# The last output quarter of a slot, evicted by the slot after it

## The chip, the cores and the metric

One core of a Trainium2 chip runs the kernel. The metric is the device time of one execution in microseconds (us). Three runs before the change took 793.52, 794.09 and 795.62 us, median 794.09. Five engines work side by side: TensorE (PE, matmuls), VectorE (DVE), ScalarE (ACT), GpSimd (POOL) and SyncE (SP). Each runs its own instructions in order and waits for the others at semaphores. SP issues the weight loads; POOL issues the indirect DMAs that gather token rows and scatter output rows.

## The reference

The reference first computes an attention with sigmoid weights (8 batches, 12 heads, 448 positions, head size 64), and then a mixture of experts on its 3584 rows of 768 numbers, with one expert of eight for each row:

```python
attn = 1 / (1 + exp(-(q @ k.T / sqrt(64) - log(448))));  x = attn @ v
logits = x @ w_gate;            e = argmax(logits)
gate = softmax(logits)[e];      eom = sigmoid(x @ w_output_gate)[e]
out = gate * eom * (maximum(x @ w1[e], 0) @ w2[e])     # w1: 768x1024, w2: 1024x768
```

## The kernel before

The attention fills the first 330 us or so. The rest is the mixture of experts, cut into slots. A slot is a set of token rows of one expert, and its code is one body. There are full slots of 256 tokens, wide slots of 192 (128 and a quarter of 64) and half slots of 128. Every product is made of three matmuls, with each operand split into a high part (an ACT cast) and the rest (a DVE subtraction): `split` writes both.

A full body (`slot`) runs in this order. SP's loads of the next slot's w1 (`load_slot`, issued in `load_w`, L525, three loads of 1 MB; each only where the expert changes). The split of the first fourth of w2 (L535 on ACT, L536 on DVE). Layer 1 in eight chunks of six matmul pairs (L579, L580), whose sum is evicted by ACT (L587) and DVE (L588); chunks go round three PSUM banks, 0, 1 and 2, so that the fourth chunk needs the first one's eviction. Then the next slot's rows are turned (`turn_x`, L561 on DVE), POOL gathers the rows of the slot after that (L504), the turned rows and w1 are split (L539, L542). Layer 2 makes four output quarters (t, n), t the half of the tokens and n the half of the columns, each of 24 matmuls (L604 to L606). ACT evicts each quarter with its gate as scale into the tile `ys[t]` (L616), and when n is 1 POOL scatters `ys[t]` to the output (L618, 128 rows of 3072 bytes). The list `lt` holds a slot's row numbers and gates.

A wide body is the same for 192 tokens, with the 64 in fp32 without a split: `layer2_q` (32 matmuls at L661, evicted at L663, scattered at L664) and two more quarters. A half body has another order, in which hidden units are transposed by PE (`turn`, L705) from a tile that ACT writes (L726).

Slots 0 to 3 always run. The rest sit in nested branches: `If(full > k)` with full bodies (L968), then `If(wide > k)` with wide ones (L973), then `If(part > k)` with half ones (L978). With these inputs 11 full slots run (7 inside branches), 3 wide ones and 2 half ones. Where a nest is left, each engine jumps on its own and adds what the bodies not run would have added to its semaphores. Its event there waits for all its own earlier work: on POOL for the landing of each of its DMAs, and then an instruction (INC_SWDGE_SEM) brings its DMA semaphores to the later count. What comes next on another engine waits for such a count wherever it depends on anything that a body of the nest may have done.

The order inside a body is the order of the code, engine by engine.

Of the kernel before, what the change touches and what calls it, by code (L numbers as in the profile page):

```python
# [12 lines left out]
I32 = mybir.dt.int32  # L13
# [9 lines left out]
E = 8  # L23
# [12 lines left out]
EARLY = -(-(ROWS_E - E * (TS - 1)) // TS)  # L36
# [18 lines left out]
def r32(ap):  # L55
    return ap.bitcast(F32)


class Kernel:
# [19 lines left out]
    def memory(self):  # L79
        self.rounded = self.pool("rounded").tile([128, ROUNDED // 4], F32R, name="rounded")  # L80
        self.plain = self.pool("plain").tile([128, PLAIN // 4], F32, name="plain")
        ps = self.pool("psum", space=PSUM).tile([128, 8, 512], F32, name="ps")
        self.ps_s = [ps[:, 0:2], ps[:, 2:4]]
        self.ps_o = [[ps[:, 4], ps[:, 5]], [ps[:, 6], ps[:, 7]]]
        self.mm_ps, self.mm_late = ps[:, 5], ps[:, 7]
        self.psx = [ps[:, i].rearrange("p (d t) -> p d t", d=2) for i in (6, 7)]
        self.psh = [ps[:, i] for i in (0, 1, 2, 4, 5)]
        self.psy = [ps[:, i] for i in (4, 5, 3)]
        self.rot = {}

        c = self.carve
        w = c(0, 3, 2, 2, DF)
        self.w1s = [[w[:, d // 2, a, d % 2] for d in range(6)] for a in range(2)]
        self.w1p = [[w[:, k, a] for k in range(3)] for a in range(2)]
        self.xc = c(12 * DF * 4, 6, 2, TS)
        self.xs = [self.xc[:, :, i] for i in range(2)]

        self.w1r = c(0, 6, DF, dt=F32)
        o = 6 * DF * 4
        self.xg = c(o, 8, Q4, dt=F32)  # L100
        self.xT = c(o + XG, 6, TS, dt=F32)
        o += 2 * XG
        self.w2r = c(o, 8, DM, dt=F32)
        self.li = c(o, LROWS, 6, dt=F32)
        self.lr_e = [c(o + LROWS * 24 + i * 768, 192, dt=F32, parts=32) for i in range(2)]
        self.tmp_early = o + 4096
        self.step = c(o + 8192, B, 4, dt=F32, parts=CP)
        self.tokf = c(o + 8192 + 16 * B, NCH, 4, dt=F32, parts=CP)
# [29 lines left out]
    def constants(self):  # L138
        nc = self.nc
        cp = self.const = self.pool("const")  # L140
# [20 lines left out]
            t, pattern=pattern, base=base, channel_multiplier=0, allow_small_or_imprecise_dtypes=True)  # L161
# [29 lines left out]
        nc.gpsimd.memset(self.seg, 1.0)  # L191
        nc.gpsimd.memset(self.seg[:, :, 0:1], 0.0)
        slots = EARLY + LATE_N
        self.lts = cp.tile([128, slots, 2, 2], I32, name="lts")
        self.lxs = cp.tile([128, slots, 8], I32, name="lxs")
        for i, st in enumerate((1, TS)):
# [4 lines left out]
        own = gl[1].bitcast(I32)  # L201
# [403 lines left out]
            nc.tensor.matmul(ps, hh[:, f, tk], wl, start=False, stop=False)  # L605
            nc.tensor.matmul(ps, hl[:, f, tk], wh, start=False, stop=(f == 7))  # L606

    def layer2(self, s, t, n, y):
        ps = self.take("y", self.psy)[:, 0:384]
        self.layer2_mm(ps, t, n, range(8))  # L610
        self.layer2_out(ps, s, t, n, y)

    def layer2_out(self, ps, s, t, n, y):
        nc = self.nc
        c = slice(384 * n, 384 * n + 384)
        nc.scalar.activation(y[:, c], ps, AF.Copy, scale=r32(s["lt"][:, t, 1:2]))  # L616
        if n == 1:
            nc.gpsimd.indirect_dma_start(  # L618
                out=self.out, out_offset=bass.IndirectOffsetOnAxis(ap=s["lt"][:, t, 0:1], axis=0),
                in_=y, in_offset=None, bounds_check=NT - 1, oob_is_err=False)  # L620

    def slot(self, m, side=None, drain=False):
        tab, k = (self.tab_e, m + 1) if m + 1 < EARLY else (self.tab_l, m + 1 - EARLY)
        nx = self.load_slot(tab, k, self.lists(m + 1))
        self.split_w2(0)
        for f in range(8):
            self.layer1(f, m == 0 and f == 0)
            if f:
                self.high_low(f - 1)
            if f in (1, 3, 5):  # L630
                self.split_w2(f // 2 + 1)
            if side is not None and f < 7:
                next(side, None)
        self.high_low(7)
        if side is not None and m == 0:
            next(side, None)
        if drain:
            self.nc.gpsimd.drain()
        self.load_w2(nx)
        self.high_w1(0)  # L640
        self.turn_x(nx)
        if m != EARLY - 2:
            self.gather(self.lists(m + 2), ROWS_E if m + 2 < EARLY else NT)
        for k in range(3):
            self.split_x(nx, k)
        self.low_w1(0)
        for i, (t, n) in enumerate(((0, 0), (0, 1), (1, 0), (1, 1))):
            self.layer2(self.lists(m), t, n, self.ys[t])
            if i < 2:
                self.split_w1(i + 1)  # L650
            if side is not None and i > 0:
                next(side, None)
        if m == EARLY - 2:
            self.gather(self.lists(m + 2))

    def layer2_q(self, s, y):
        nc = self.nc
        ps = self.take("y", self.psy)[:, 0:384]
        for f in range(8):
            for n in range(2):  # L660
                nc.tensor.matmul(ps[64 * n:64 * n + 64], self.hq[:, f], self.w2r[:, f, 384 * n:384 * n + 384],  # L661
                                 start=(f == 0), stop=(f == 7))
        nc.scalar.activation(y[:, 0:384], ps, AF.Copy, scale=r32(s["lq"][:, 1:2]))  # L663
        nc.gpsimd.indirect_dma_start(  # L664
            out=self.out.rearrange("t (n c) -> (t n) c", n=2),
            out_offset=bass.IndirectOffsetOnAxis(ap=s["lq"][:, 0:1], axis=0),
            in_=y[:, 0:384], in_offset=None, bounds_check=2 * NT - 1, oob_is_err=False)

    def wide_slot(self, j):
        cur = self.wide_lists(j)  # L670
        nx = self.load_slot(self.tab_l, LATE_F + j + 1, self.wide_lists(j + 1))
        self.split_w2(0)
        for f in range(8):
            self.layer1(f, n=WS)
            if f:
                self.high_low(f - 1, HS)
            if f in (1, 3, 5):
                self.split_w2(f // 2 + 1)
        self.high_low(7, HS)
        self.high_w1(0)  # L680
        self.turn_x(nx)
        self.gather(self.wide_lists(j + 2))
        for k in range(3):
            self.split_x(nx, k)
        self.low_w1(0)
        self.layer2_q(cur, self.ys[1])
        self.load_w2(nx)
        self.split_w1(1)
        self.layer2(cur, 0, 0, self.ys[0])
        self.split_w1(2)  # L690
        self.layer2(cur, 0, 1, self.ys[0])

    def half_slot(self, j, y):
        nc = self.nc
        nx = None
        if j + 1 < E:
            nx = self.load_slot(self.tab_b, j + 1, self.half_lists(j + 1))
        if j:
            nc.gpsimd.drain()  # L699
        (wh, wl), (xh, xl), (hh, hl) = self.w1s, self.xs, self.hs  # L700

# [9 lines left out]
        for n in range(2):  # L711
            c = slice(512 * n, 512 * n + 512)
            ps = self.take("h", self.psh)
# [13 lines left out]
            if n == 0:  # L727
                nc.scalar.copy(w2[2][1], w2[2][0])
        cur = dict(lt=self.ltb[:, j])
        pss = [self.take("y", self.psy)[:, 0:384] for n in range(2)]  # L730
        self.layer2_mm(pss[0], 0, 0, range(2))
        turn(1)
        if nx is not None:
# [167 lines left out]
    def build(self, phases="abc"):  # L901
        tc, nc = self.tc, self.nc
# [56 lines left out]
        for m in range(EARLY + LATE_MIN):  # L959
            if m == EARLY + LATE_MIN - 1:  # L960
# [4 lines left out]
                part = nc.values_load(self.tot[0:1, 2:3], min_val=0, max_val=E)  # L965
# [7 lines left out]
        with ExitStack() as ctx:  # L973
            for k in range(E):
                ctx.enter_context(tc.If(wide > k))
                with tc.manual_schedule():
                    self.wide_slot(k)
        with ExitStack() as ctx:  # L978
            for k in range(E):
                ctx.enter_context(tc.If(part > k))  # L980
                with tc.manual_schedule():
                    self.half_slot(k, self.ys[k % 2])


@with_exitstack
# [34 lines left out]
```

## Time and profile before

| | |
|---|---|
| runs without a profile | 793.52, 794.09, 795.62 us |
| the profiled execution, and its span | 799.36 us, 797.6 us |
| PE busy | 771.8 us (97% of the span) |
| DVE, ACT, POOL busy | 498.2, 490.0, 330.4 us (62%, 61%, 41%) |
| moved by DMA | 145.61 MB, 183 GB/s on the mean |

The times in a trace are those of one profiled execution, counted from the start of its span; its own time is 799.36 us. A row of the timeline has the start, the duration, the engine, the line of the kernel, what is written from what, and in brackets how long the engine sat idle before it and what it then waited for. An engine name with a q at its end (ACTq) is the engine's sequencer, which handles branches and semaphores. "Issue" is time that no wait explains.

### The profile page before, as it was taken

The page shows a single profiled execution, that of the slowest core. Times are in us where ns is not written, and L with a number is a line of the kernel's source. Part 1 is how long each engine was busy: PE and PEld are TensorE (multiplying, and loading weights), DVE is VectorE, ACT ScalarE, POOL GpSimd, SP SyncE. Part 2 cuts the span into 40 slices and gives each one's busy share as a digit, 9 for nine tenths or more (in the row PEclk, how much of TensorE's full clock was granted, in tenths as well). Part 3 has the DMA queues.
Part 4 walks back from the last instruction along what each step waited for, and adds up shares of the span by engine and source line. Part 5 has one row for each costly group of instructions (what it writes and reads, how often), then busy time and mean ns, then how long its engine had stood idle before and what let it go on. Part 6 is the DMA issues. An engine that isn't in the chain of part 4 may idle for free. (4 is left out here: it accounts for less than half of the span.)

```text
span 797.6 us, 15037 instructions
## 1 busy us (share of the span) xinstructions
PE 771.8 (97%) x5724; PEld 564.3 (71%) x5724; DVE 498.2 (62%) x779; ACT 490.0 (61%) x662; POOL 330.4 (41%) x468
## 2 busy tenths in 40 slices
PE   9999999999999999899999999999999998999893
PEld 4333433333333379799899999999999997888773
DVE  3344435434456668977685775857758575787685
ACT  5666666666668556465574565745657464667674
POOL 4003302320333475657836626345162551543453
PEclk9999999999999999999999999999999999999997
DMA  6353453425458350247468776521165835956861
GB/s 255 133 209 123 163 203 140 180 100 209 150 168 344 110 179 6 80 147 240 184 232 295 236 252 243 169 68 31 50 236 174 299 114 204 349 219 237 288 239 44
DMA packets 37807, 145.61 MB, mean 183 GB/s; under 512 B 5703, under 2 KB 7919, under 8 KB 33744
## 3 DMA queue, kind: packets, MB, share of 16 engines
q1 hardware_dynamic: 27696, 119.56, 42.3%
q0 software_dynamic: 10016, 24.85, 9.4%
q8 instruction: 51, 0.84, 0.4%
q14 instruction: 44, 0.36, 0.2%
HBM read 153.00 MB, written 23.05 MB: 221 GB/s over the span
## 5 line engine op out<-in xcount | busy, mean ns | idle before, releaser
L579 PE MATMUL ps<-rounded 128*128 128x512 f32 (+1 forms) x672 | 229.3, 390 | 5.1 <-ACTq L968 2.9
L504 POOL DMA_INDIRECT plain<-x_dram,lxs x122 | 170.5, 1398 | 151.0 <-DVE plain L561 109.4
L782 ACT ACTIVATE a<-ps,bias_s 128x896 f32<-128x896 f32 x168 | 169.0, 1007 | 101.7 <-PE ps L780 95.2
L580 PE MATMUL ps<-rounded 128*128 128x256 f32 (+1 forms) x672 | 185.3, 276 | 0.9 <-DVE rounded L542 0.9
L536 DVE TENSOR_TENSOR w2l<-plain,w2h 128x1536 fp32r<-128x1536 f32 x60 | 105.3, 1757 | 96.3 <-ACT w2h L535 63.8
L780 PE MATMUL ps<-kqv 64*64 64x448 f32 x1344 | 159.3, 540 | 1.4 <-issue 0.6
L789 PE MATMUL ps<-a,kqv 64*64 64x448 f32 x1344 | 157.4, 536 | 0.0
L579 PEld LDWEIGHTS ps<-rounded 128*128 128x128 f32 x672 | 127.5, 190 | 29.5 <-ACTq L968 3.2
L604 PE MATMUL ps<-w2h,h 128*128 128x384 f32 x432 | 144.8, 335 | 0.0
L606 PE MATMUL ps<-w2h,h 128*128 128x384 f32 x432 | 144.4, 334 | 0.0
L605 PE MATMUL ps<-w2l,h 128*128 128x384 f32 x432 | 144.3, 334 | 0.0
L580 PEld LDWEIGHTS ps<-rounded 128*128 128x128 f32 x672 | 128.9, 192 | 1.2 <-DVE rounded L542 1.2
L542 DVE TENSOR_TENSOR rounded<-plain,rounded 128x2048 fp32r<-128x2048 f32 x46 | 103.7, 2285 | 6.2 <-ACT rounded L539 4.6
L789 PEld LDWEIGHTS ps<-a,kqv 64*64 64x64 f32 x1344 | 52.3, 133 | 74.5 <-issue 73.3
L780 PEld LDWEIGHTS ps<-kqv 64*64 64x64 f32 x1344 | 49.1, 133 | 75.8 <-issue 63.5
L535 ACT CAST w2h<-plain 128x1536 fp32r<-128x1536 f32 x60 | 88.1, 1472 | 10.6 <-PE ps L819 4.4
L539 ACT CAST rounded<-plain 128x2048 fp32r<-128x2048 f32 x46 | 87.5, 1902 | 0.0
L587 ACT COPY gl<-ps 128x256 f32<-128x256 f32 (+1 forms) x112 | 40.2, 359 | 70.2 <-PE ps L580 59.7
L604 PEld LDWEIGHTS ps<-w2h,h 128*128 128x128 f32 x432 | 81.1, 188 | 2.3 <-issue 1.8
L605 PEld LDWEIGHTS ps<-w2l,h 128*128 128x128 f32 x432 | 81.1, 188 | 0.1
L606 PEld LDWEIGHTS ps<-w2h,h 128*128 128x128 f32 x432 | 81.1, 188 | 0.0
L616 ACT ACTIVATE y<-ps,lts 128x384 f32<-128x384 f32 x50 | 29.0, 580 | 69.3 <-PE ps L606 49.6
(206 smaller groups left out, 691.4 us busy)
## 6 DMA issues: line engine op xcount, KB each, us to landing
plain<-w SPq DMA_DIRECT2D x68, 768.0 KB
plain<-w SPq DMA_DIRECT2D x48, 1024.0 KB
kqv<-kqv SPq DMA_DIRECT2D x23, 1344.0 KB
x_dram<-xt SPq DMA_DIRECT2D x8, 1344.0 KB
plain<-w SPq DMA_DIRECT2D x6, 512.0 KB
plain<-x_dram,lxs POOLq DMA_INDIRECT x122
kqv<-kqv SPq DMA_DIRECT2D x1, 896.0 KB
lst<-plain POOLq DMA_DIRECT2D x1, 726.0 KB
```

The source lines that it names most:

```text
L504: self.nc.gpsimd.indirect_dma_start(out=s["xg"][:, g], out_offset=None, in_=x4, in_offset=bass.IndirectOffsetOnAxis(ap=s["lx"][:, g:g + 1] ...
L535: self.nc.scalar.copy(hi, raw)
L536: self.nc.vector.tensor_tensor(lo, raw, r32(hi), ALU.subtract)
L542: self.nc.vector.tensor_tensor(self.w1p[1][k], self.w1r[:, 2 * k:2 * k + 2], r32(self.w1p[0][k]), ALU.subtract)
L579: nc.tensor.matmul(out, wh[d][:, c], both, start=(d == 0), stop=False)
L580: nc.tensor.matmul(ps[:, 0:n], wl[d][:, c], self.xc[:, d, 0, 0:n], start=False, stop=(d == 5))
L604: nc.tensor.matmul(ps, hh[:, f, tk], wh, start=(f == 0), stop=False)
L605: nc.tensor.matmul(ps, hh[:, f, tk], wl, start=False, stop=False)
L606: nc.tensor.matmul(ps, hl[:, f, tk], wh, start=False, stop=(f == 7))
L780: nc.tensor.matmul(ps[half[h], j, 0:S], kg[half[j], e, 0, o:o + 64], kg[half[j], e, 1], start=True, stop=True)
L782: nc.scalar.activation(at[u % 4], ps[:, :, 0:S], AF.Sigmoid, bias=self.bias_s, scale=1.0 / math.sqrt(D))
L789: nc.tensor.matmul(self.ps_o[e][h][half[j], 0:S], v[half[h], 6 if i == 3 else 3 * e + c, j], a[half[h], j], start=(i in ((0, 3 if h else 4 ...
```

## The change

For slots from 3 on (`m >= EARLY`), the last quarter (1, 1) always goes to PSUM bank 3. DVE copies its row numbers and gates to a small tile `due`. ACT's eviction and POOL's scatter of that quarter (`finish`) are moved to the start of whatever body runs next: a full one, a wide one, the first half one, or the Else branch where there is no half slot. The other quarters use fixed banks 4, 5, 4. In wide bodies the same holds for the quarter (0, 1); the splits of w1 stand ahead of `layer2_q`, and `layer2_q` uses `ys[0]`, the quarters `ys[1]`.

```diff
-        self.psy = [ps[:, i] for i in (4, 5, 3)]
+        self.psy = [ps[:, i, 0:384] for i in (4, 5, 3)]
+        self.due = cp.tile([128, 2], I32, name="due")
...
-    def layer2(self, s, t, n, y):
-        ps = self.take("y", self.psy)[:, 0:384]
+    def layer2(self, s, t, n, y, ps):
         self.layer2_mm(ps, t, n, range(8))
         self.layer2_out(ps, s, t, n, y)
+
+    def layer2_due(self, s, t):
+        own, v = s["lt"][:, t], self.nc.vector
+        v.tensor_copy(self.due[:, 0:1], own[:, 0:1])
+        v.tensor_copy(r32(self.due[:, 1:2]), r32(own[:, 1:2]))
+        self.layer2_mm(self.psy[2], t, 1, range(8))
+
+    def finish(self):
+        self.layer2_out(self.psy[2], dict(lt=self.due.unsqueeze(1)), 0, 1, self.ys[1])
...
     def slot(self, m, side=None, drain=False):
         nx = self.load_slot(tab, k, self.lists(m + 1))
+        if m > EARLY:
+            self.finish()
         self.split_w2(0)
...
-            self.layer2(self.lists(m), t, n, self.ys[t])
+            if i == 3 and m >= EARLY:
+                self.layer2_due(self.lists(m), 1)
+            else:
+                ps = self.psy[(0, 1, 0)[i] if m >= EARLY else (4 * m + i) % 3]
+                self.layer2(self.lists(m), t, n, self.ys[t], ps)
...
     def wide_slot(self, j):
         nx = self.load_slot(self.tab_l, LATE_F + j + 1, self.wide_lists(j + 1))
+        self.finish()
         self.split_w2(0)
...
-        self.layer2_q(cur, self.ys[1])
+        self.split_w1(1)
+        self.split_w1(2)
+        self.layer2_q(cur, self.ys[0])
         self.load_w2(nx)
-        self.split_w1(1)
-        self.layer2(cur, 0, 0, self.ys[0])
-        self.split_w1(2)
-        self.layer2(cur, 0, 1, self.ys[0])
+        self.layer2(cur, 0, 0, self.ys[1], self.psy[1])
+        self.layer2_due(cur, 0)
 
     def half_slot(self, j, y):
-        if j:
+        if j == 0:
+            self.finish()
+        else:
             nc.gpsimd.drain()
...
+        with tc.If(part > 0) as some:
+                self.half_slot(0, self.ys[0])
+                for k in range(1, E):
+                    ctx.enter_context(tc.If(part > k))
+                        self.half_slot(k, self.ys[k % 2])
+        with some.Else():
+                self.finish()
```

The first place is ACT where the full bodies are left and the first wide one begins. Before, L616 is an eviction, L968 the exit of the full nest with its event, L973 the entry of the wide one, L535 the first split of w2 and L587 the evictions of layer 1. In brackets stands what an instruction waits for; DMASW are POOL's DMAs.

```order
L616 ACTIVATE y_2464<-ps,lts 128x384 [waits PE_49]
L539 CAST rounded<-plain 128x2048 [waits DMAHW2_49]
L616 ACTIVATE y_2465<-ps,lts 128x384 [waits DMASW4_49,PE_49]
L616 ACTIVATE y_2465<-ps,lts 128x384 [waits PE_49]
L968 UNCONDITIONAL_BRANCH
L968 UNCONDITIONAL_BRANCH [waits Activation_49] x11
L973 COMPARE_AND_BRANCH
L535 CAST w2h<-plain 128x1536 [waits DMAHW3_49,DMAHW2_49,DMAHW4_49,DMAHW1_49,DMAHW5_49,DMAHW0_49,DMAHW6_49,DVE_49,DMAHW7_49,PE_49,Activation_49]
L587 COPY gl_103<-ps 128x192 [waits DVE_49,PE_49,Activation_49] x2
```

The same place of the changed kernel, whose lines have other numbers: L625 is the eviction, L986 and L991 the exit and the entry, L536 the split and L588 the evictions of layer 1.

```order
L625 ACTIVATE y_2465<-ps,lts 128x384 [waits PE_49]
L540 CAST rounded<-plain 128x2048 [waits DMAHW2_49]
L625 ACTIVATE y_2466<-ps,lts 128x384 [waits DMASW4_49,PE_49]
L986 UNCONDITIONAL_BRANCH
L986 UNCONDITIONAL_BRANCH [waits Activation_49] x11
L991 COMPARE_AND_BRANCH
L625 ACTIVATE y_2466<-ps,due 128x384 [waits DMASW2_49,DMASW0_49,DMASW4_49,DVE_49,DMASW6_49,PE_49,Activation_49]
L536 CAST w2h<-plain 128x1536 [waits DMAHW4_49,DMAHW3_49,DMAHW5_49,DMAHW2_49,DMAHW6_49,DMAHW1_49,DMAHW7_49,DMAHW0_49,Activation_49]
L588 COPY gl_104<-ps 128x192 [waits PE_49,Activation_49] x2
```

The last eviction has moved from ahead of the exit to behind the entry, and there it stands ahead of the split and waits for four of POOL's DMA semaphores.

The second place is the same exit on POOL. Before, the last full body ends with a gather and two scatters; the ISA row of the exit is INC_SWDGE_SEM.

```order
L504 DMA plain<-x_dram,lxs 128x192 [waits DMASW4_49]
L618 DMA out<-y_2464,lts 3584x768 [waits DMASW5_49,Activation_49]
L618 DMA out<-y_2465,lts 3584x768 [waits DMASW6_49,DMASW5_49,Activation_49]
L968 UNCONDITIONAL_BRANCH
L968 ISA [waits DMASW4_49,DMASW5_49,DMASW3_49,DMASW6_49,DMASW2_49,DMASW7_49,DMASW1_49,DMASW0_49]
```

These two scatters and all gathers are what the exit's last row waits for. In the changed kernel (L505 the gather, L627 the scatter) the same body ends so:

```order
L505 DMA plain<-x_dram,lxs 128x192
L505 DMA plain<-x_dram,lxs 128x192 [waits DMASW4_49]
L627 DMA out<-y_2465,lts 3584x768 [waits DMASW5_49,Activation_49]
L986 UNCONDITIONAL_BRANCH
L986 ISA [waits DMASW4_49,DMASW5_49,DMASW3_49,DMASW6_49,DMASW2_49,DMASW7_49,DMASW1_49,DMASW0_49]
```

The second scatter has left the work that the exit waits for. It now opens the first wide body on POOL, behind the nest's entry L991:

```order
L991 COMPARE_AND_BRANCH
L627 DMA out<-y_2466,due 3584x768 [waits DMASW4_49,DMASW3_49,DMASW5_49,DMASW2_49,DMASW6_49,DMASW1_49,DMASW7_49,DMASW0_49,Activation_49]
L505 DMA plain<-x_dram,lxs 128x192 [waits DMASW3_49,DVE_49]
L505 DMA plain<-x_dram,lxs 128x192 [waits DMASW6_49,DMASW4_49]
L505 DMA plain<-x_dram,lxs 128x192 [waits DMASW7_49]
```

It stands there ahead of the wide body's gathers and waits for ACT's moved eviction.

## Rows read from the trace of the kernel before

**Rows 1.** Waits of PE: line, what it waited for, total us, times, longest
```profile
PE ps L579 <- ACTq L968: 2.9, 1, 2.9
PE ps L720 <- PEq L973: 2.7, 1, 2.7
```

**Rows 2.** Timeline of PE, first wide slot
```profile
661.17 0.59 PE L579 MATMUL ps<-rounded 128*128 128x384 f32 x1 [2.86 <-ACTq L968]
...
664.39 0.52 PE L579 MATMUL ps<-rounded 128*128 128x384 f32 x1
...
676.59 1.83 PE L661 MATMUL ps<-plain,hb 128*64 128x384 f32 x10
```

**Rows 3.** Line L968, 650 to 680 us: ns min/median/max, first and last start
```profile
L968 POOLq EVENT_SEMAPHORE  x4: 17/43/43, 664.4 to 673.2; - x4
...
L968 DVEq EVENT_SEMAPHORE  x1: 21/21/21, 655.5 to 655.5; - x1
L968 PEldq EVENT_SEMAPHORE  x1: 51/51/51, 658.8 to 658.8; - x1
L968 ACTq EVENT_SEMAPHORE  x1: 17/17/17, 661.1 to 661.1; - x1
L968 POOLq INC_SWDGE_SEM  x1: 1801/1801/1801, 673.3 to 673.3; - x1
```

**Rows 4.** Timeline of ACT, from the full slots to the wide ones
```profile
654.19 0.58 ACT L616 ACTIVATE y<-ps,lts 128x384 f32<-128x384 f32 x1 [1.77 <-PE ps L606]
658.35 0.58 ACT L616 ACTIVATE y<-ps,lts 128x384 f32<-128x384 f32 x1 [3.58 <-issue]
661.80 1.47 ACT L535 CAST w2h<-plain 128x1536 fp32r<-128x1536 f32 x1 [2.87 <-ACTq L968]
```

**Rows 5.** Timeline of DVE, first wide slot
```profile
663.30 1.76 DVE L536 TENSOR_TENSOR w2l<-plain,w2h 128x1536 fp32r<-128x1536 f32 x1 [8.57 <-ACT w2h L535]
665.03 0.35 DVE L588 TENSOR_TENSOR gl<-gl,ps 128x192 f32<-128x192 f32 x1
```

**Rows 6.** Timeline of POOL, last scatters of the full slots
```profile
659.61 1.00 POOL L618 DMA_INDIRECT out<-y,lts  x1 [0.30 <-issue]
664.16 1.77 POOL L618 DMA_INDIRECT out<-y,lts  x1 [3.55 <-ACT w2h L535]
```

**Rows 7.** Line L618, 645 to 664 us, columns as in rows 3
```profile
L618 POOLq EVENT_SEMAPHORE  x2: 17/6340/12663, 648.2 to 650.7; - x2
```

**Rows 8.** Line L525 (weight loads), 655 to 680 us, columns as in rows 3
```profile
L525 SPq DMA_DIRECT2D plain<-w x5: 377/377/386, 661.1 to 679.4; - x5
```

**Rows 9.** Waits of SP, columns as in rows 1
```profile
SPq L525 <- ACTq L968: 5.5, 1, 5.5
```

**Rows 10.** Windows: length, busy us by engine, PE clock, DMA share, GB/s
```profile
661.00:672.00 11.00, 10.82 (x65) 10.83 (x66) 5.64 (x12) 5.94 (x10) 1.77 (x1) 0.84 0.95 347
```

**Rows 11.** Line L973 (exit of the wide slots), columns as in rows 3
```profile
L973 POOLq EVENT_SEMAPHORE  x4: 17/43/8242, 751.6 to 760.0; - x4
...
L973 POOLq INC_SWDGE_SEM  x1: 2253/2253/2253, 760.1 to 760.1; - x1
```

**Rows 12.** Line L978 (exit of the half slots), columns as in rows 3
```profile
L978 POOLq INC_SWDGE_SEM  x1: 278/278/278, 795.6 to 795.6; - x1
```

**Rows 13.** Timeline of POOL around the exit of the wide slots
```profile
751.65 1.16 POOL L618 DMA_INDIRECT out<-y,lts  x1 [3.53 <-ACT w2h L535]
```

**Rows 14.** Line L618, 745 to 756 us, columns as in rows 3
```profile
L618 POOLq EVENT_SEMAPHORE  x1: 17/17/17, 750.9 to 750.9; - x1
```

**Rows 15.** Timeline of ACT, first half slot
```profile
748.67 2.86 ACT L535 CAST w2h<-plain 128x1536 fp32r<-128x1536 f32 x2 [2.63 <-issue]
752.47 0.60 ACT L726 ACTIVATE hb<-ps 128x512 f32<-128x512 f32 x1 [0.95 <-PE ps L722]
```

**Rows 16.** Timeline of PE, first half slot
```profile
754.32 0.60 PE L705 MATMUL ps<-ident,hb 128*128 128x128 f32 x4
```

**Rows 17.** Timeline of DVE, first half slot
```profile
762.73 0.98 DVE L561 STREAM_TRANSPOSE plain<-plain 128x768 f32<-128x768 f32 x1 [2.47 <-DMA plain<-x_dram,lxs]
```

More of the change, by code (lines that the diff above doesn't have):

```diff
@@ L657, in layer2_q @@
         nc = self.nc
-        ps = self.take("y", self.psy)[:, 0:384]
+        ps = self.psy[0]
         for f in range(8):
@@ L729, in half_slot @@
         cur = dict(lt=self.ltb[:, j])
-        pss = [self.take("y", self.psy)[:, 0:384] for n in range(2)]
+        pss = self.psy[0:2]
         self.layer2_mm(pss[0], 0, 0, range(2))
@@ L977, in build @@
                     self.wide_slot(k)
[L978 to L982, printed above, removed]
+        with tc.If(part > 0) as some:
+            with tc.manual_schedule():
+                self.half_slot(0, self.ys[0])
+            with ExitStack() as ctx:
+                for k in range(1, E):
+                    ctx.enter_context(tc.If(part > k))
+                    with tc.manual_schedule():
+                        self.half_slot(k, self.ys[k % 2])
+        with some.Else():
+            with tc.manual_schedule():
+                self.finish()
 @with_exitstack
```

## The prediction

> **What bounds the kernel now.** I read the waits of PE first. Its two longest are at the places where a nest is left: 2.9 us for ACT's exit between the full and the wide slots, and 2.7 us for its own sequencer between the wide and the half ones [rows 1]. From one full slot to the next, where most of the edit acts, it does not wait at all. So time changes where PE waits or would wait, and in the tail behind PE's last matmul, which POOL ends. I read these places next: the exit rows, then the timelines of ACT, DVE and POOL beside them.
>
> At the first exit PE ended at 658.31 and began again at 661.17 [rows 2]. ACT's last eviction began at 658.35, its exit event came at 661.1 [rows 3, 4], 2.75 us later. PE's own event was at 658.8, DVE's at 655.5 [rows 3]. So only ACT's late eviction held PE. After that gap the first six matmul pairs took 3.22 us up to 664.39. The remaining 42 took 12.2 us up to 676.59 [rows 2], 0.29 us each, 1.74 us a chunk of six. The window of 661 to 672 shows a granted clock of 0.84 [rows 10]: PE ran at 1.2 GHz instead of 2.4 for a while, which cost some 1.5 us.
>
> **The change, part by part.** Inside a nest the moved eviction stands where it stood, at the end of the slot's last matmul and ahead of the next split; the scatter was issued in the next body before, too. DVE's two copies of 128x1 lie in its idle time before the turn (8.57 us of it at this one [rows 5]). I cost these at nothing; without that cover each would be less than the 0.35 us of an addition of 192 columns [rows 5]. The earlier splits of w1 in wide slots move work between engines that PE does not wait for there: nothing as well. What is left are the two exits.
>
> *The gain at the first exit.* ACT's last eviction ahead of its exit is now that of the third quarter, at 654.19 [rows 4]; plus 2.75 its exit event comes at about 656.9. PE then waits for its own exit (658.8, and some 0.6 us of jumps and events) and restarts near 659.5, 1.7 us earlier. A gap of 1.2 us may spare the slow clock, another 1.5.
>
> *What takes the place of the wait.* The moved eviction now is ACT's first instruction of the wide body, and the order shows that it waits for four of POOL's DMA semaphores. The counts that it wants are reached only when POOL's exit adds what the bodies not run would have added. Before, nothing at the head of ACT's wide body did: the cast there ran at 661.80 [rows 4], while POOL's exit ended only at 673.3 + 1.8 = 675.1 [rows 3]. Behind the eviction on ACT are queued the split of w2 and all evictions of layer 1, and with three banks PE can run only three chunks ahead.
>
> When does POOL's exit end? It waits for the landing of the scatter that is left, issued at 659.61 [rows 6]. Before, that landed at 650.7 + 12.66 = 663.4 [rows 7], 3.8 us after its start. But then SP's three weight loads began only at 661.1 [rows 8], since the first of them waited 5.5 us for ACT's exit [rows 9]. With ACT's exit at 656.9 they come 4.2 us sooner: 2.6 us ahead of the scatter instead of 1.5 behind it. Both scatters that were issued behind such loads took long: 664.16 to 673.2, 9.0 us [rows 3, 6], while the DMA engines were 95% busy [rows 10]; and 751.65 to 760.0, 8.4 us [rows 11, 13]. I take 8.7: landing at 668.3; the ends are 3.8 and 9.0, so 663.4 and 668.6. INC_SWDGE_SEM took 1.80 and 2.25 us at these two exits and 0.28 at the end of the kernel [rows 3, 11, 12]; I take 2.0, since the first two are exits of the same kind. With 0.1 for the events the eviction starts at 670.4 (663.8 to 671.0).
>
> From there the fourth chunk needs the first chunk's eviction: 0.58 for the moved one, 1.47 for the cast [rows 4], 1.76 for DVE's subtraction, 0.35 for the addition [rows 5], about 4.1 with their overlaps. So PE goes on at 674.5. Having restarted at 659.5 and done three chunks of 1.74, it has then stood for some 9.8 us. Five chunks follow, 8.7 us, to 683.2; with the slow clock again 684.7. Before it was 676.59: +6.6 to +8.1. I take **+7.2**. With the low ends layer 1 ends at 676.6, nothing lost; with the high ones and the slow clock at 685.3, +8.7.
>
> *The exit of the wide slots.* PE's 2.7 us are its own sequencer's and stay. The exit of POOL now waits for the scatter of the 64 tokens, landed by 750.9 [rows 14], instead of the one that landed at 760.0. With 1.8 to 2.25 us for INC_SWDGE_SEM it ends at 752.8 to 753.2 instead of 762.4 (751.3 with 0.28). But ACT's moved eviction waits for it there too: where the casts began at 748.67 and the relu (L726) at 752.47 [rows 15], the eviction (0.58), two casts (2.86) and the relu (0.60) now end at about 756.7 to 757.1. PE's transposes, at 754.32 [rows 16], wait for this: +2.4 to +2.8 (0.9 at the low end). Up to 0.5 may be added at the second four transposes. On the other side the turn of the rows, at 762.73 after 2.47 us of waiting for POOL's exit [rows 17], was ready at 760.26; from it hang POOL's gathers and so the end of the kernel. 760.26 plus PE's new delay is 762.7 to 763.1, so the tail moves by 0 to +0.4; I take **+0.3**, with ends of -1.6 and +0.9.
>
> The sum is +7.5 us: the profiled 799.36 would become 806.9. That execution lies 5.3 us above the median of the runs without a profile; the difference carries over: 794.09 + 7.5 = **801.6**. The ends of the terms give 792.5 to 803.7.
>
> **Rivals.** *A fast landing.* The scatter lands in 3.8 us in spite of the loads, as it did before. The eviction then starts at 663.4 + 0.1 + 2.0 = 665.5, PE goes on at 669.6, and layer 1 ends at 678.3 to 679.8: +1.7 to +3.2, with the tail +2 to +3.5, about 797. For it: both short landings [rows 7, 14]. Against it: those had their loads behind them, and this one has them ahead. The Trainium skill (DMA: Bandwidth & Descriptors, Anatomy of one DMA — SWDGE (gpsimd) path) gives 2.0 us plus bytes by 436 GB/s for one DMA, an estimate of 2.9 us for these 393 KB after the issue. By that rule this rival would hold, and the time be about 797. The trace agrees for the scatter of 659.61 (3.8 us with its 1.0 of issue), and not for that of 664.16 with the same bytes (9.0).
>
> *Only the gain.* The moved eviction does not wait, for instance because its counts are reached already. Then PE restarts 1.7 us sooner, keeps its clock (1.5), and the turn comes at 760.3 rather than 762.73 (2.4): -5.6, 788.5. For it: the old eviction there waited only for PE. Against it: the waits in the order, and the turn's 2.47 us, which show that such a count is really waited for [rows 17].
>
> *A backlog.* ACT and DVE, 9 us late, do not catch up in the five chunks that are left; layer 2 then waits for their splits of w2 as well. Two chunks need two casts' worth of this chain, some 3.8 us (1.47, 1.76 and the two additions with their evictions), against 3.5 on PE. Over five chunks and the four splits that is 2 to 3 us more: about 804.5.
>
> **How the numbers follow.** I give the forecast 0.60, the fast landing 0.22, the gain alone 0.08, the backlog 0.10. About 0.3% (2.4 us, 791.7 to 796.5) is what a measurement of this kernel can tell from no change. Slower than that are the forecast, the backlog and nearly half of the fast landing: 0.80. The lower part of the fast landing, with a short INC_SWDGE_SEM, is no change: 0.12. Faster is 0.08. The likeliest case alone runs from 799 to 803.7; the range that holds the others to all but two in ten is 795.5 to 805.
>
> **What would show it.** In the profile after: ACT's exit event near 657 and the weight loads with it; PE's first wide matmul near 659.5 after a gap of about 1.2 us; then a wait of PE of about 10 us in the fourth chunk, with the moved eviction as the end of it, and that starting right behind INC_SWDGE_SEM near 670. In the first half slot a wait of 2 to 3 us at the transposes, and a turn that no longer waits for POOL. I am wrong if the wide slots' first eviction starts before 664, if the scatter lands within 5 us, or if PE's new wait lies somewhere else.

## The result, and the profile after

The changed kernel took 803.89 us (median of 4, 803.14 to 805.89) against 794.17 us before (median of 4): a ratio of 1.0118, 95% interval 1.0093 to 1.0144, so 7.4 to 11.4 us slower. The span of its profiled execution is 801.4 us, only 3.8 us above that of before. The two part ways earlier, in code that the change leaves alone: in the attention the execution before lost 4.5 us.

The windows of before around that place (length, busy us by engine, PE clock, DMA share, GB/s):

```profile
260.00:265.00 5.00, 3.62 (x21) 0.77 (x13) 3.42 (x5) 1.01 (x1) 4.00 (x10) 1.00 0.29 80
```

And of the changed kernel:

```profile
260.00:265.00 5.00, 5.00 (x52) 1.87 (x52) 3.30 (x7) 2.65 (x3) 4.04 (x4) 1.00 0.28 72
```

PE was busy for 3.6 of these 5 us before and ran 21 matmuls; after, it was busy for all of them and ran 52. The last full slot's last matmul (the first wide matmul's start less its gap) ends at 658.31 before and at 653.85 after, 4.5 us apart, and the loss in the attention is all of that. So I compare the profiles from this end to the end of the span: 797.6 - 658.31 = 139.3 us before [rows 2], 801.4 - 653.85 = 147.6 after, +8.3.

The waits of PE after the change:

```profile
PE ps L580 <- DVE gl L589: 10.8, 2, 8.6
PE ps L723 <- ACT hb L744: 2.6, 1, 2.6
PE ps L738 <- PEq L991: 1.8, 1, 1.8
...
PE ps L580 <- PEq L986: 1.2, 1, 1.2
```

ACT's 2.9 us of [rows 1] have gone. In their place stand 1.2 us for PE's own exit and a wait of 8.6 us for an eviction of layer 1. The other 2.2 us of the first row were there before:

```profile
PE ps L579 <- DVE gl L588: 2.2, 1, 2.2
```

The exit of the full slots (L986 was L968), in the columns of [rows 3]:

```profile
L986 POOLq EVENT_SEMAPHORE  x4: 17/42/43, 660.8 to 662.8; - x4
...
L986 DVEq EVENT_SEMAPHORE  x1: 21/21/21, 650.4 to 650.4; - x1
L986 ACTq EVENT_SEMAPHORE  x1: 17/17/17, 652.2 to 652.2; - x1
L986 PEldq EVENT_SEMAPHORE  x1: 51/51/51, 654.3 to 654.3; - x1
L986 POOLq INC_SWDGE_SEM  x1: 1781/1781/1781, 662.9 to 662.9; - x1
```

ACT leaves at 652.2, ahead of PE at 654.3. POOL leaves last, at 662.9 + 1.78 = 664.7. ACT's timeline, to be held against [rows 4]:

```profile
649.73 0.58 ACT L625 ACTIVATE y<-ps,lts 128x384 f32<-128x384 f32 x1 [1.77 <-PE ps L607]
664.87 0.58 ACT L625 ACTIVATE y<-ps,due 128x384 f32<-128x384 f32 x1 [14.56 <-DMA plain<-x_dram,lxs]
665.35 1.46 ACT L536 CAST w2h<-plain 128x1536 fp32r<-128x1536 f32 x1
```

The moved eviction starts 0.2 us behind POOL's exit, after ACT has stood for 14.6 us, and the cast starts behind it. The row puts the wait down to a gather of POOL's, which had long been issued; that it was POOL's exit is read from the two times here, and tested below. PE, to be held against [rows 2]:

```profile
655.02 0.41 PE L580 MATMUL ps<-rounded 128*128 128x384 f32 x1 [1.17 <-PEq L986]
668.92 0.69 PE L580 MATMUL ps<-rounded 128*128 128x384 f32 x1 [8.56 <-DVE gl L589]
...
674.37 0.46 PE L580 MATMUL ps<-rounded 128*128 128x384 f32 x1
...
680.26 1.19 PE L676 MATMUL ps<-plain,hb 128*64 128x384 f32 x6
```

Three chunks, a wait of 8.56 us, five chunks. The first ten pairs behind the wait take 5.45 us up to 674.37; the window shows the clock at half:

```profile
669.00:674.40 5.40, 5.40 (x21) 5.40 (x21) 3.43 (x10) 3.92 (x7) 0.00 (x0) 0.50 0.01 3
```

Layer 1 ends 680.26 - 653.85 = 26.4 us after the last full slot; before, 676.59 - 658.31 = 18.3. That is +8.1 of the +8.3 us: 8.56 of waiting and 2.6 of slow clock behind it (ten pairs at full clock take 2.9 us), less 1.7 by the shorter gap and the 1.5 that the slow clock cost before, some 8.0 in all.

The scatter that POOL's exit waits for, and the weight loads (L526 was L525), to be held against [rows 6, 8]:

```profile
655.16 1.00 POOL L627 DMA_INDIRECT out<-y,lts  x1 [0.30 <-issue]
```

```profile
L526 SPq DMA_DIRECT2D plain<-w x8: 372/372/381, 652.2 to 688.0; - x8
```

The loads start with ACT's exit at 652.2, 3.0 us ahead of the scatter, and that has landed by POOL's last exit event at 662.8, 7.6 us after its start instead of 3.8.

### The profile page after: what moved, and what is told of

The parts are those of the page before. It is cut to its first block, busy times and chain, and to the rows that moved or that the text cites. A ratio compares the mean times of both kernels' runs of the same rounds, so it can differ in the third digit from the quotient of the medians.

```text
span 801.4 us, 15073 instructions
## 1 busy us (share of the span) xinstructions
PE 771.8 (96%) x5724; PEld 565.6 (71%) x5724; DVE 499.3 (62%) x801; ACT 488.8 (61%) x662; POOL 325.6 (41%) x468
## 5 line engine op out<-in xcount | busy, mean ns | idle before, releaser
L580 PE MATMUL ps<-rounded 128*128 128x512 f32 (+1 forms) x672 | 230.4, 391 | 12.0 <-DVE gl L589 10.8
L505 POOL DMA_INDIRECT plain<-x_dram,lxs x122 | 167.7, 1375 | 159.0 <-DVE plain L562 117.4
L580 PEld LDWEIGHTS ps<-rounded 128*128 128x128 f32 x672 | 128.2, 191 | 36.6 <-DVE gl L589 12.1
L605 PE MATMUL ps<-w2h,h 128*128 128x384 f32 x432 | 145.0, 336 | 0.7 <-ACT y L625 0.7
L536 ACT CAST w2h<-plain 128x1536 fp32r<-128x1536 f32 x60 | 87.9, 1469 | 5.1 <-PE ps L837 4.4
L588 ACT COPY gl<-ps 128x256 f32<-128x256 f32 (+1 forms) x112 | 40.2, 360 | 65.6 <-PE ps L581 59.3
L301 POOL TENSOR_TENSOR pos<-pc,off 112x32 f32<-112x32 f32 x8 | 3.8, 473 | 143.6 <-ACT pc L299 143.6
```

The costliest lines, as they stand in the source:

```text
L505: self.nc.gpsimd.indirect_dma_start(out=s["xg"][:, g], out_offset=None, in_=x4, in_offset=bass.IndirectOffsetOnAxis(ap=s["lx"][:, g:g + 1] ...
L536: self.nc.scalar.copy(hi, raw)
L580: nc.tensor.matmul(out, wh[d][:, c], both, start=(d == 0), stop=False)
L605: nc.tensor.matmul(ps, hh[:, f, tk], wh, start=(f == 0), stop=False)
```

## The experiments

Each was timed beside the kernel before on the same chip. The kernel before took 799.89 us there (median) beside the one that is late in the half slot and the 30 added matmuls, 797.71 beside the repetition and the 46 added matmuls, and 800.38 beside the others, against 794.17 above; so the runs are compared by their ratios. The traces are compared by the time from the last full matmul to the end of the span, as above; differences there are to the 139.3 us before.

| | ratio to before (95%) | last full matmul to end, us | PE's wait in the fourth chunk of the first wide slot, us |
|---|---|---|---|
| changed kernel | 1.0118 (1.0093 to 1.0144) | 147.6, +8.3 | 8.6 |
| late in both | 0.9926 (0.9898 to 0.9954) | 132.8, -6.5 | none |
| late in both, again | 0.9922 (0.9895 to 0.9948) | 135.2, -4.1 | none |
| late in the wide slot | 0.9957 (0.9933 to 0.9981) | 136.4, -2.9 | none |
| late in the half slot | 1.0091 (1.0061 to 1.0121) | 145.0, +5.7 | 8.6 |
| only the order of the splits | 0.9981 (0.9963 to 0.9999) | 138.9, -0.4 | none |
| no loads in the first wide slot | 1.0067 (1.0042 to 1.0091) | 144.9, +5.6 | 4.5 |
| 30 added matmuls | 1.0136 (1.0082 to 1.0190) | 147.3, +8.1 | 3.4 |
| 46 added matmuls | 1.0165 (1.0125 to 1.0205) | 146.5, +7.2 | 0.6 |

**The moved eviction late, in both first bodies.** By then POOL's exit is over: in the first wide slot it ends at 669.0 + 1.78 = 670.8, and the eviction starts 6 us later.

```profile
L989 POOLq INC_SWDGE_SEM  x1: 1781/1781/1781, 669.0 to 669.0; - x1
```

```profile
677.05 0.57 ACT L625 ACTIVATE y<-ps,due 128x384 f32<-128x384 f32 x1
```

```diff
 def wide_slot(self, j):
-        self.finish()
+        if j:
+            self.finish()
...
         self.high_low(7, HS)
+        if j == 0:
+            self.finish()
 def half_slot(self, j, y):
-        if j == 0:
-            self.finish()
-        else:
+        if j:
             nc.gpsimd.drain()
...
+        if j == 0:
+            self.finish()
         pss = self.psy[0:2]
```

> The changed kernel, with the moved eviction and scatter (finish) placed behind layer 1 in the first wide slot and behind the second relu in the first half slot, instead of at the head; in all other slots it stays at the head. Theory (the moved eviction waits for POOL's exit, and PE with it): by then POOL's exit is over, so the 8.6 us wait of PE in the fourth chunk and the 2.6 us at the transposes are gone, PE restarts about 1.7 us sooner than in the kernel before and keeps its clock (1.5), and the turn of rows no longer waits for POOL (2.4): 794.2 - 4 to 6 = 788 to 790. Rival (fixed banks, copies on DVE or the order of the splits cost the time): it stays at 800 to 804.

Measured: 0.9926, and 0.9922 on another chip, 5.9 and 6.2 us under the kernel before. PE's timeline of the first wide slot:

```profile
661.01 0.41 PE L580 MATMUL ps<-rounded 128*128 128x384 f32 x1 [1.05 <-PEq L989]
674.81 5.38 PE L676 MATMUL ps<-plain,hb 128*64 128x384 f32 x32
```

Eight chunks in 13.8 us behind a gap of 1.05, at full clock throughout. This is the change with its price taken away, and it beats both kernels. The rival is out: all of the change's other parts are in this kernel.

> The kernel with the moved eviction late in the first wide and the first half slot once more, on this chip, beside the same runs of the kernel before: 0.9926 again within 0.3%, if its gain is the first exit's 3.2 us and the tail's 2.4 us.

The ratio came again; the trace shows only -4.1 us, since in that execution PE stood for 2.60 us at the second exit, 0.8 more than in the first trace, and ran at half clock for a while behind it, which cost 1.6 more. Its first matmul there, and the window:

```profile
743.00 0.47 PE L739 MATMUL ps<-rounded 128*128 128x512 f32 x1 [2.60 <-issue]
```

```profile
743.00:746.00 3.00, 3.00 (x9) 2.39 (x10) 1.99 (x2) 2.35 (x2) 0.00 (x0) 0.66 0.73 193
```

**Late in one body alone.** The first half of the diff above, and the second.

> The same for the first wide slot alone; in the first half slot the eviction stays at the head. Theory: the first exit's loss turns into the gain of 1.7 + 1.5 us, the wait of 2.6 us at the transposes stays and the tail is as in the changed kernel (+0.1): about 791. Rival (the loss comes from the half slots or from the other parts): 800 or more.

> The changed kernel with the moved eviction late in the first half slot alone; in the first wide slot it stays at the head. Theory: the 2.6 us of PE at the transposes go and the turn of rows comes sooner, as between the kernels with it late in both and in the wide slot alone (2.5 us), while the loss at the first exit stays: about 2.5 us under the changed kernel, ratio to before about 1.009. Rival (the two places work on the same time, since POOL's chain at the end hides one of them): no difference from the changed kernel.

Measured: 0.9957 (-3.4 us) and 1.0091 (+7.3). Late in the wide slot alone, the half slot's wait stays:

```profile
PE ps L726 <- ACT hb L747: 2.9, 1, 2.9
```

The two places add up: late in the half slot is worth 0.27% from the changed kernel and 0.31% from the one that is late in the wide slot; late in the wide slot is worth 1.6%. So the loss sits at the first exit. The second seems to cost a little, too: each of the two differences of 0.3% is no larger than the intervals are wide, but they agree, and the three pairs of traces have 2.6, 3.6 and 1.2 us (of the 2.6, 1.1 lie at the first exit, where fewer pairs were slow).

**The order of the splits alone**, on the kernel before.

```diff
+        self.split_w1(1)
+        self.split_w1(2)
         self.layer2_q(cur, self.ys[1])
         self.load_w2(nx)
-        self.split_w1(1)
         self.layer2(cur, 0, 0, self.ys[0])
-        self.split_w1(2)
```

> The kernel before, with only the splits of w1 ahead of layer2_q in the wide slots. Theory: these move work of ACT and DVE that PE does not wait for; 794.2 within 0.3%, the waits of PE as before. Rival (the order of the splits makes the loss, since the eviction of layer2_q and its scatter come later): 798 to 804.

Measured: 0.9981, within 0.3%, and PE's waits for ACT's exit stay. The order of the splits makes none of the loss. Its trace shows one thing more, at the first exit:

```profile
661.99 0.44 PE L579 MATMUL ps<-rounded 128*128 128x384 f32 x1 [2.95 <-ACTq L968]
675.82 5.38 PE L661 MATMUL ps<-plain,hb 128*64 128x384 f32 x32
```

The same wait as before, 2.95 us, and no slow clock behind it: 13.83 us for the eight chunks, not 15.42 [rows 2].

**No weight loads in the first wide slot.** The second wide slot computes with the first one's w1, and its output is left so.

```diff
-    def load_slot(self, tab, k, s):
+    def load_slot(self, tab, k, s, load=True):
         s = dict(s, **self.slot_regs(tab, k))
-        self.load_w(s, self.w1, self.w1r, range(0, 6, 2))
+        if load:
+            self.load_w(s, self.w1, self.w1r, range(0, 6, 2))
...
-        nx = self.load_slot(self.tab_l, LATE_F + j + 1, self.wide_lists(j + 1))
+        nx = self.load_slot(self.tab_l, LATE_F + j + 1, self.wide_lists(j + 1), load=j > 0)
```

> The changed kernel without the three loads of w1 in the first wide slot, so that the second wide slot computes with the w1 of the first. Theory (the scatter that POOL's exit waits for lands late because the loads now run ahead of it): it lands in about 3.8 us instead of 7.6, the eviction starts 3.8 us sooner after the last full slot, PE's wait shrinks from 8.6 to about 4.8 us: about 800. Rival (the landing or the exit is slow for another reason): the wait stays at 8.6 us and the time at 803.9.

The scatter, its landing (the last of POOL's exit events) and PE, from its trace:

```profile
659.44 1.00 POOL L628 DMA_INDIRECT out<-y,lts  x1 [0.31 <-issue]
```

```profile
L987 POOLq EVENT_SEMAPHORE  x4: 17/43/43, 661.9 to 663.0; - x4
...
L987 POOLq INC_SWDGE_SEM  x1: 1781/1781/1781, 663.1 to 663.1; - x1
```

```profile
669.08 0.69 PE L581 MATMUL ps<-rounded 128*128 128x384 f32 x1 [4.54 <-DVE gl L590]
```

It lands 3.6 us after its start, POOL's exit and the end of PE's wait both come 4.0 us sooner after the last full slot, and the ratio falls from 1.0118 to 1.0067, some 4 us. So about half of PE's wait is the collision of the scatter with the loads that the earlier exit let loose. The rest would be there without it. Of the 4.0 us the end of the trace keeps 2.7 (+5.6 where the changed kernel has +8.3), mainly since PE ran at half clock for longer in the first half slot: at 0.50 from 763 to 766 us, where the changed kernel was at 1.00 from 764 on.

**Matmuls added in the wait**, to see what the slow clock costs.

```diff
         for f in range(8):
             self.layer1(f, n=WS)
+            if j == 0 and f == 2:
+                self.warm(30)
...
+    def warm(self, n):
+        ps, wh = self.psy[1], self.w1s[0]
+        for i in range(n):
+            both = self.xc[:, i % 6, :, 0:WS]
+            out = ps.rearrange("p (a t) -> p a t", a=2)
+            self.nc.tensor.matmul(out, wh[i % 6][:, 0:128], both, start=True, stop=True)
```

> The changed kernel with 30 more matmuls of 384 columns on PE behind the third chunk of the first wide slot, written to a bank that is overwritten later: PE works through most of the 8.6 us in which it now waits. Theory (2.6 us of the loss is the slow clock after the wait: ten pairs took 5.45 us instead of 2.87): the clock stays at 2.4 GHz in the fourth and fifth chunk, and the time is some 2.5 us less than that of the changed kernel, if the added matmuls end before the eviction that PE waits for: ratio to before about 1.009. Rival (the evictions of ACT and DVE set the pace of the last five chunks anyway): the clock is full and the time the same as the changed kernel's, 1.012.

> The changed kernel with 46 instead of 30 added matmuls of 384 columns behind the third chunk of the first wide slot: with 30 of 0.18 us PE still stood for 3.4 us and the slow clock came after that. 46 take 8.3 us and leave about 0.5 us. Theory (the slow clock is a part of the loss, 2.6 us): no slow pairs in the last five chunks, layer 1 of that slot ends 23.8 us after the last full slot instead of 26.4, ratio to before about 1.009. Rival (ACT and DVE set the pace of these chunks anyway): full clock, but new waits of PE between the chunks, and 26 us as in the changed kernel.

The 30 were too few: 3.4 us of waiting were left, and slow pairs came behind them. With 46, PE's timeline reads:

```profile
662.86 8.19 PE L618 MATMUL ps<-rounded 128*128 128x384 f32 x46
671.63 0.44 PE L580 MATMUL ps<-rounded 128*128 128x384 f32 x1 [0.58 <-DVE gl L589]
...
675.44 0.44 PE L580 MATMUL ps<-rounded 128*128 128x384 f32 x1 [0.15 <-DVE gl L589]
...
681.11 5.38 PE L683 MATMUL ps<-plain,hb 128*64 128x384 f32 x32
```

No slow pair is left, layer 1 ends 681.11 - 656.45 = 24.7 us after the last full slot instead of 26.4, and PE now waits between the chunks for evictions. So in the trace the clock is worth 1.7 of the 2.6 us, and ACT and DVE take the rest: both theories have a share. The times without a profile do not show it: both kernels came out slower than the changed one, 1.0136 and 1.0165, with intervals that overlap its own. In the profile of the first, PE stood for 6.0 us at another place, in the routing ahead of the slots:

```profile
PE ps L275 <- issue: 6.0, 1, 6.0
```

Whether the longer program brings such stalls in the other executions, too, is open; the verdict on the clock rests on one trace.

## Why the prediction was right

The time lies in the range, 2.3 us over the forecast of 801.6, and by the mechanism that was forecast. Of the 2.3 us the traces have 0.8 (+8.3 where +7.5 was forecast); the other 1.5 stand in the runs alone, and no trace shows where they lie. By the steps of the forecast:

- *Inside the nest, nothing.* Right: PE does not wait between full slots, and the first exit starts from the same place in the trace once the 4.5 us in the attention are taken off. The splits alone changed nothing that can be told. The 8.57 us of [rows 5] are DVE's idle time ahead of the split of w2, not of the turn as I wrote; the two copies are nothing all the same, 0.15 and 0.14 us at the first exit with 16.4 us of idle time behind them.
- *The gain at the exit.* The gap of 1.2 us came as 1.17. ACT's exit event followed the start of its last eviction by 2.5 us (2.75 forecast). The clock stayed full behind the gap.
- *The wait for POOL's exit.* Right: the eviction began 0.2 us behind it, and putting it late took the wait away. From the last full matmul to the eviction it was 11.0 us (12.1 forecast): the landing took 7.6 us, not 8.7, and INC_SWDGE_SEM 1.78, not 2.0.
- *Eviction to fourth chunk.* 668.92 - 664.87 = 4.05 us, forecast 4.1. PE's wait was 8.6 us, forecast 9.8, by the 1.1 us of the step above.
- *The last five chunks.* Mis-sized: 11.3 us instead of 8.7 to 10.2. I had carried over the six slow pairs of [rows 2]; after the longer wait ten pairs were slow. The two misses cancel in part: +8.1 at the end of layer 1 where +7.2 was taken, at the upper end of its +6.6 to +8.1.
- *The half slots.* The wait at the transposes came as 2.64 us (2.4 to 2.8 forecast). Behind it PE ran at half clock, which was not forecast: the first four transposes took 1.11 us instead of 0.60 [rows 16]. PE's own exit cost 1.8 instead of 2.7 us. The tail moved by 8.3 - 8.1 = 0.2 us, forecast 0.3, and that is luck in part: the turn came 8.8 us later after the last full slot (113.2 instead of 104.4), 0.6 more than layer 1, and POOL's rows from the turn to the start of its last scatter took 0.6 less, 28.8 instead of 29.4.

The rows of the changed kernel that show the half slot's part are ACT's moved eviction, the transposes, POOL's exit, the turn and the last scatter, to be held against [rows 11, 15, 16, 17]:

```profile
756.04 0.58 ACT L625 ACTIVATE y<-ps,due 128x384 f32<-128x384 f32 x1 [10.47 <-DMA plain<-x_dram,lxs]
```

```profile
759.90 1.11 PE L723 MATMUL ps<-ident,hb 128*128 128x128 f32 x4 [2.64 <-ACT hb L744]
```

```profile
L991 POOLq INC_SWDGE_SEM  x1: 2233/2233/2233, 753.6 to 753.6; - x1
```

```profile
767.04 0.97 DVE L562 STREAM_TRANSPOSE plain<-plain 128x768 f32<-128x768 f32 x1
```

```profile
795.87 1.00 POOL L627 DMA_INDIRECT out<-y,gl  x1 [0.30 <-issue]
```

The last scatter before:

```profile
792.16 1.00 POOL L618 DMA_INDIRECT out<-y,gl  x1 [0.30 <-issue]
```

POOL's exit is over at 755.8, the eviction starts 0.2 us later, PE's transposes follow it, and the turn no longer waits for POOL, but comes 16.2 us after PE's first matmul of the half slot (750.88) instead of 14.6 (after 748.10).

The rival of a fast landing is refuted for this kernel (7.6 us), and its landing shown to be what would be without the loads ahead (3.6 us); layer 1 still ended 22.1 us after the last full slot there, +3.8 where this rival had +1.7 to +3.2. The time by the Trainium skill's formula (DMA: Bandwidth & Descriptors, Anatomy of one DMA — SWDGE (gpsimd) path), an estimate of 2.9 us, comes near there (3.6 us, of which 1.0 are POOL's issue) and not beside the loads (7.6 with the same 1.0). The backlog exists in small: with the clock kept full, PE waited again for evictions in the last chunks. The gain alone, -5.6 us, came once the eviction was put late: -5.9 and -6.2.

## What to carry to other kernels

Work that is moved across a branch's exit takes on waits for the exits of other engines that it depends on. Here POOL left last, 10.8 us after PE's last matmul, and set its time; look at what is queued behind such work. Put it where the last exit is over and nothing short of buffers stands behind it: the same edit went from 1.2% slower to 0.7% faster that way. An engine that leaves earlier also lets loads start earlier, and these can hold up the very DMA that the slow exit waits for (7.6 us to its landing with them, 3.6 without).

## What was not expected of the hardware

The slow clock after a gap of PE is not a matter of the gap's length alone at this size. It came behind waits of 2.86 us [rows 2], 2.60 (late in both, again) and 2.02 (late in the half slot), and did not behind 2.95 (only the splits) or at the exit of the wide slots behind 2.7 [rows 1]. PE ran the same code ahead of the 2.86 and of the 2.95. The wait of 2.02, and the window behind it with a granted clock of 0.65:

```profile
754.21 0.47 PE L736 MATMUL ps<-rounded 128*128 128x512 f32 x1 [2.02 <-issue]
```

```profile
754.00:757.00 3.00, 2.79 (x8) 2.25 (x9) 1.78 (x2) 2.56 (x2) 0.76 (x1) 0.65 0.59 128
```

Behind 8.56 us it was there in both kernels that had such a wait, for ten pairs in one; in the other, the one that is late in the half slot, the last five chunks took 683.37 - 673.18 = 10.2 us instead of 11.3.

```profile
673.18 0.69 PE L580 MATMUL ps<-rounded 128*128 128x384 f32 x1 [8.56 <-DVE gl L589]
...
683.37 5.38 PE L676 MATMUL ps<-plain,hb 128*64 128x384 f32 x32
```

So a gain from a shorter gap of two to three us is a chance, not a sum: the 1.5 us that I counted as possible at the first exit were there to be won in the execution of the kernel before, and not in that of the kernel with only the order of the splits changed.
